# One table of tokens by expert split into two, the first block's rows turned later, and the probabilities stored as 18 rows

## The chip, the core and the metric

The kernel runs on one core of one Trainium2 chip. A core has TensorE (PE, matmuls and transposes), VectorE (DVE), ScalarE (ACT), GpSimd (POOL) and SyncE (SP), which here only issues DMAs and loads registers. Each takes its own instructions strictly in the order in which the program hands them out and waits on the others by semaphores. The metric is the device time of one execution in microseconds.

## The reference

Three stages follow one another: attention with pooled queries, a mixing layer with a gate, and a routed layer in which each token goes to one of eight experts.

```python
def _moe2_ref(x, w_gate, w_local, w1, w2):        # x: (4, 576, 512)
    logits = np.einsum('bsd,de->bse', x, w_gate)
    local_gate = 1.0 / (1.0 + np.exp(-np.einsum('bsd,de->bse', x, w_local).squeeze(-1)))
    for b in range(B):
        prev_e = -1
        for s in range(S):
            fresh_e = int(np.argmax(logits[b, s]))
            if s == 0 or local_gate[b, s] < 0.5:
                e = fresh_e
            else:
                e = prev_e if prev_e >= 0 else fresh_e
            prev_e = e
            p = ...                               # softmax of logits[b, s]
            h = np.maximum(x[b, s] @ w1[e], 0.0)
            out[b, s] = p[e] * (h @ w2[e])
```

Before it, `_attn_ref` averages pairs of queries and computes softmax(q k / 8) v, and `_moe_ref` mixes each token with the one before it, computes relu(xk w_k) squared times w_v, and multiplies by sigmoid(xr w_r). There are 2304 tokens of 512 numbers.

## The kernel before

The attention comes first and is not touched but for its constants. The 2304 tokens of the mixing layer are worked in 9 pairs `u` of tiles of 128 tokens. From u = 2 to u = 7 a loop does one round each: `hidden(u+1, 0..1)`, `gate(u, 0)`, `route2(u-1)`, the mixing of pair u+2, `value(u, 0)`, `product(u, 0)`, `route3(u-1)`, `logits(u, 0)`, `gate(u, 1)`, `route4(u-1)`, `value(u, 1)`, `product(u, 1)`, `logits(u, 1)`, `hidden(u+1, 2..3)`, `route1(u)`. The pair u = 8 is written out behind the loop.

Routing: `logits` are nine multiply-and-add passes on DVE (line 783). `route1` (DVE) takes the largest logit and makes `kg` (line 822), the gate and candidate of each token; `route2` turns `kg` into a row on PE (line 832), ACT copies it to `krow` (line 836), and a scan on DVE gives the expert of every token as `erow` (line 838). `route3` spreads it on PE (line 849) and DVE makes the one-hot `oh` (line 850). `route4` counts with matmuls of `oh` (lines 857 to 861), DVE adds up the slots to `base` (lines 863 to 869), and POOL writes the token numbers `tid` of the two tiles into the DRAM table `tbl` by two indirect DMAs (line 871). The table has a list of 2816 places for each expert; places not written hold 2304, an index that means "no token". A hidden group's squares go from ACT (lines 745 to 747) to POOL, which makes the low half (line 748); the low half of the mixed tokens is POOL's as well (line 568).

The routed layer goes in blocks of up to 512 tokens of one expert. `early()` takes the expert with the most tokens of the first 14 tiles as block 0, before the routing is complete. For a block, `load_ids` (line 1015, SP) loads 512 token numbers from the table, `gather_x` (lines 1027, 1029, POOL) fetches these tokens' rows by indirect DMA, two tiles of 128 at a time, `transpose_x` turns them on PE (line 1054) with copies by ACT and DVE (lines 1057, 1058), `load_w` and `split_w` load 8 pieces of weights and split them into a high and a low half (lines 988, 994; 1010, 1011), and `up`/`down` multiply (lines 1068, 1085). `gather_p` (line 1037, POOL) fetches the tokens' probabilities from the DRAM tensor `pd`, which `probabilities()` writes: 18 numbers on each of 128 partitions, as single numbers (line 1217). `finish` (lines 1093, 1094) scales and stores.

SP's DMAs run on a set of eight completion counters, used in turn; an issue can thus wait for the DMA eight issues before it. Ahead of block 1 SP loads the registers of all later blocks, 28 register loads between the store of the probabilities and the next weights.

## Time and profile before

| | |
|---|---|
| three runs | 1199.29, 1200.1 (median), 1203.38 us |
| profiled execution | 1199.74 us, its span 1198.0 us |
| PE busy | 1080.2 us (90% of the span) |
| DVE, ACT, POOL busy | 828.2, 718.6, 575.3 us |
| mean granted TensorE clock, whole span | 0.972 of full speed |
| the same from 830 to 870 us, 870 to 910, 910 to 950 | 0.85, 0.90, 0.91 |
| the same from 950 to 1070 us | 1.00 |

The views in order of time give the start and length of merged instructions, and in square brackets how long the engine sat idle before the first of them and what ended that. The view of waits adds the same idle times up by the pair of instructions. Idle time of an engine costs only where PE, the busiest one, or the end of the program waits for it in turn.

### The profile page before, as it was taken

The numbers are of one execution on the slowest core, as the hardware profiler recorded it, in microseconds if no ns is written. First come the engines' busy times: TensorE is split into PE (matmuls) and PEld (weight loads), VectorE is DVE, ScalarE is ACT, GpSimd is POOL, SyncE is SP. The second block draws the span as 40 slices with busy tenths as digits, with TensorE's granted clock in tenths as the row PEclk, the third lists the DMA queues.
The fourth block names the chain that finished last, engine by engine and source line by source line (L and its number), as shares of the span: only waits on it lengthen the run. The fifth ranks groups of instructions, "written<-read, shape, count | busy, mean of one in ns | idle before, by whom it ended". The sixth has DMA issues, their size and how long they took to land. (4 is left out here: it accounts for less than half of the span.)

```text
span 1198.0 us, 18084 instructions
## 1 busy us (share of the span) xinstructions
PE 1080.2 (90%) x6073; PEld 910.6 (76%) x6073; DVE 828.2 (69%) x1255; ACT 718.6 (60%) x1006; POOL 575.3 (48%) x392
## 2 busy tenths in 40 slices
PE   7899999999999999978999989897987999998875
PEld 6677777777777777767887878776776888876764
DVE  6888888888888888889955665685353544446544
ACT  5787777777777777767775444341333535446543
POOL 2556666666666666468734333342213514144233
PEclk9999999999999999998999999998897999999988
DMA  9166666656566564515520322203646756556765
GB/s 198 32 132 148 138 142 141 140 130 131 131 149 141 137 138 100 157 45 172 182 98 10 36 31 32 36 18 89 117 81 153 253 178 202 176 179 213 251 205 176
DMA packets 147348, 156.31 MB, mean 130 GB/s; under 512 B 62993, under 2 KB 115857, under 8 KB 146324
## 3 DMA queue, kind: packets, MB, share of 16 engines
q1 hardware_dynamic: 140836, 141.51, 47.4%
q0 software_dynamic: 6384, 13.15, 3.7%
q8 instruction: 73, 1.20, 0.5%
q14 instruction: 55, 0.45, 0.1%
HBM read 107.30 MB, written 15.58 MB: 103 GB/s over the span
## 5 line engine op out<-in xcount | busy, mean ns | idle before, releaser
L403 PE MATMUL pvt<-sr,V 128*128 128x288 f32 x1152 | 328.5, 409 | 31.4 <-ACT xc L416 14.7
L403 PEld LDWEIGHTS pvt<-sr,V 128*128 128x128 f32 x1152 | 202.1, 190 | 71.2 <-POOL sr L389 17.9
L345 PE MATMUL pt<-kw 128*128 128x288 f32 x1152 | 247.3, 337 | 5.5 <-DVE Mt L357 4.1
L389 POOL TENSOR_TENSOR sr<-sr,Mb 128x576 f32<-128x576 f32 x96 | 142.5, 1487 | 195.3 <-ACT Mb L380 159.5
L357 DVE TENSOR_TENSOR Mt<-Mt,pt 128x576 f32<-128x576 f32 x224 | 168.1, 750 | 76.2 <-ACT sr L349 74.3
L349 ACT ACTIVATE sr<-pt 128x576 f32<-128x576 f32 x288 | 181.5, 646 | 54.6 <-PE pt L345 52.4
L345 PEld LDWEIGHTS pt<-kw 128*128 128x128 f32 x1152 | 177.6, 189 | 34.8 <-DVE Mt L357 10.4
L396 ACT ACTIVATE sr<-sr 128x1728 f32<-128x1728 f32 x96 | 157.9, 1644 | 52.0 <-DVE sr L390 46.4
L390 DVE TENSOR_TENSOR sr<-sr,Mb 128x1152 f32<-128x1152 f32 x96 | 160.9, 1676 | 2.8 <-ACT Mb L380 2.8
L727 PE MATMUL ph<-a,wk 128*128 128x256 f32 x864 | 108.4, 286 | 0.9 <-ACT kr L745 0.4
L727 PEld LDWEIGHTS ph<-a,wk 128*128 128x128 f32 x864 | 106.5, 193 | 2.6 <-ACT kr L745 1.0
L767 PE MATMUL py<-kw,sq 128*128 128x512 f32 x312 | 84.3, 423 | 0.0
L1068 PE MATMUL ph<-a,wk 128*128 128x256 f32 x576 | 73.4, 288 | 6.3 <-PEq L1415 5.8
L1085 PE MATMUL py<-kw,sq 128*128 128x512 f32 x324 | 78.3, 398 | 0.0
L1068 PEld LDWEIGHTS ph<-a,wk 128*128 128x128 f32 x576 | 71.3, 195 | 8.8 <-issue 7.7
L871 POOL DMA_INDIRECT tbl<-tid,si x18 | 18.4, 1021 | 122.9 <-DMA tbl<-tid,si 67.2
L745 ACT ACTIVATE kr<-ph 128x512 f32<-128x512 f32 x36 | 21.3, 592 | 92.4 <-PE ph L727 57.2
L446 POOL TENSOR_TENSOR xo<-xc,t 64x576 f32<-64x576 f32 x32 | 73.1, 2283 | 1.2
L783 DVE CUSTOM_DVE_ANT_0 a<-r,wg 128x512 f32<-128x512 f32 x96 | 71.4, 744 | 3.1
L767 PEld LDWEIGHTS py<-kw,sq 128*128 128x128 f32 x312 | 62.1, 203 | 15.0 <-issue 0.2
L1085 PEld LDWEIGHTS py<-kw,sq 128*128 128x128 f32 x324 | 60.8, 189 | 14.5
L1037 POOL DMA_INDIRECT pg<-pd,ids x44 | 44.4, 1009 | 37.4 <-DMA pg<-pd,ids 15.7
(250 smaller groups left out, 1756.7 us busy)
## 6 DMA issues: line engine op xcount, KB each, us to landing
wraw<-in_moe_w_dram SPq DMA_DIRECT2D x101, 512.0 KB
kw<-Hk SPq DMA_DIRECT2D x224, 72.0 KB
ql<-in_q_dram SPq DMA_DIRECT2D x16, 576.0 KB
kl<-in_k_dram SPq DMA_DIRECT2D x64, 144.0 KB
V<-in_v_dram SPq DMA_DIRECT2D x128, 72.0 KB
kw<-Hq SPq DMA_DIRECT2D x112, 72.0 KB
kw<-kw SPq DMA_DIRECT2D x14, 576.0 KB
xTd<-xo SPq DMA_DIRECT2D x16, 288.0 KB
```

The costliest lines, as they stand in the source:

```text
L345: nc.tensor.matmul(pt[:, i, :HT], lhsT=lhs, rhs=qh[:, hl, hd, i, :], start=(hl == 0), stop=(hl == 1))
L349: nc.scalar.activation(out=Sg[h, kt], in_=ptt[h, kt][:, :, :HT], func=AF.Copy)
L357: nc.vector.tensor_tensor(out=Mt[h], in0=a, in1=pt[:, :, :HT], op=ALU.max)
L389: nc.gpsimd.tensor_tensor(out=s[:, 0], in0=s[:, 0], in1=Mb[h], op=ALU.subtract)
L390: nc.vector.tensor_tensor(out=s[:, 1:3], in0=s[:, 1:3], in1=Mb[h].unsqueeze(1).to_broadcast([P, 2, T]), op=ALU.subtract)
L396: nc.scalar.activation(out=s, in_=s, func=AF.Exp, scale=scale)
L403: nc.tensor.matmul(pvt[h][:, i, :HT], lhsT=V[(h // 2) % 2][:, kt, c : c + P], rhs=Sg[h, kt][:, i], start=(kt == 0), stop=(kt == KT - 1),)
L446: nc.gpsimd.tensor_tensor(out=xo[p].rearrange("p (i t c) -> p i c t", i=2, c=9)[a], in0=y[a], in1=t2[a], op=ALU.mult)
L727: nc.tensor.matmul(pt[:, i], lhsT=wk[:, wl, g, c, P * i : P * i + P], rhs=a[:, xl, c], start=(n == 0), stop=(n == 11))
L767: nc.tensor.matmul(p_v, lhsT=SQ[u, f // 2][:, xl, f % 2, s], rhs=wv[:, wl, f], start=(f == 0 and n == 0), stop=(f == 7 and n == 2),)
L1068: nc.tensor.matmul(pt[:, i], lhsT=w[:, wl, g, c, P * i : P * i + P], rhs=x[:, xl, c], start=(n == 0), stop=(n == 11))
L1085: nc.tensor.matmul(py[i], lhsT=hs[:, xl, f, P * i : P * i + P], rhs=w[:, wl, 2 * g + f], start=(g == 0 and n == 0), stop=(g == 3 and n == 5),)
```

## The change

There are two DRAM tables, `tbl[0]` for the even tiles of a pair and `tbl[1]` for the odd ones. Table 0 is filled with 2304, table 1 with 0, and the token numbers of odd tiles are stored less 2304, so the sum of the two tables is the list of before. `load_ids` loads both lists, the second into one of two new tiles `idb`, and POOL adds them in front of a block's first gather. The turning of block 0's first rows and the gather of its other rows move from in front of `route2` of pair 7 to behind `product(8, 0)`. The probabilities are turned on PE into 18 rows of 128 numbers, copied by DVE and stored as rows; this store is issued behind the last products of block 0's first half instead of ahead of POOL's gathers.

```diff
     xTd = dram.tile([DM, NTOK], F32, name="xTd")
     x2d = dram.tile([NTOK + 1, DM], F32, name="x2d")
     pd = dram.tile([NTOK + 1, 1], F32, name="pd")
-    tbl = dram.tile([E * NTS, 1], I32, name="tbl")
+    tbl = [dram.tile([E * NTS, 1], I32, name=f"tbl{i}") for i in range(2)]
 
     ctx.enter_context(tc.manual_schedule())
 
...
     nks = cp.tile([1, 8], I32, name="nks")
     wgt = cp.tile([P, 4, E + 1], F32, name="wgt")
     ids = [cp.tile([P, 4], I32, name=f"ids{i}") for i in range(4)]
+    idb = [cp.tile([P, 4], I32, name=f"idb{i}") for i in range(2)]
     pgs = [cp.tile([P, 4], F32, name=f"pg{i}") for i in range(2)]
 
     io = dict(allow_small_or_imprecise_dtypes=True)
...
         nc.gpsimd.iota(im8, pattern=[[1, E]], base=-E, channel_multiplier=0, **io)
         nc.gpsimd.iota(base, pattern=[[NTS, E]], base=0, channel_multiplier=0, **io)
         nc.gpsimd.iota(base0, pattern=[[NTS, E]], base=0, channel_multiplier=0, **io)
-        nc.gpsimd.iota(tid, pattern=[[P, NT]], base=0, channel_multiplier=1)
+        nc.gpsimd.iota(
+            tid.rearrange("p (u i) -> p u i", i=2), pattern=[[2 * P, NU], [P - NTOK, 2]], base=0, channel_multiplier=1
+        )
         nc.gpsimd.iota(k128, pattern=[[-P, 4 * NK]], base=0, channel_multiplier=0, **io)
         nc.gpsimd.iota(i4, pattern=[[1, 4]], base=1, channel_multiplier=0, **io)
         nc.gpsimd.iota(cc, pattern=[[1, NC]], base=0, channel_multiplier=0, **io)
...
         nc.vector.tensor_scalar(out=om, in0=mus, scalar1=-1.0, scalar2=1.0, op0=ALU.mult, op1=ALU.add)
         pad = tp.tile([P, E * NTS // P], I32, name="pad")
         nc.gpsimd.memset(pad, NTOK)
-        nc.sync.dma_start(tbl.rearrange("(p f) o -> p (f o)", p=P), pad)
+        nc.sync.dma_start(tbl[0].rearrange("(p f) o -> p (f o)", p=P), pad)
+        pad0 = tp.tile([P, E * NTS // P], I32, name="pad0")
+        nc.gpsimd.memset(pad0, 0)
+        nc.sync.dma_start(tbl[1].rearrange("(p f) o -> p (f o)", p=P), pad0)
         z = tp.tile([1, DM], F32, name="z")
         nc.gpsimd.memset(z, 0.0)
         nc.sync.dma_start(x2d[NTOK : NTOK + 1, :], z)
...
         nc.vector.tensor_tensor(out=base, in0=base, in1=p3[:, 2], op=ALU.add)
         for i in range(2):
             nc.gpsimd.indirect_dma_start(
-                out=tbl, out_offset=bass.IndirectOffsetOnAxis(ap=si[:, i : i + 1], axis=0),
+                out=tbl[i], out_offset=bass.IndirectOffsetOnAxis(ap=si[:, i : i + 1], axis=0),
                 in_=tid[:, 2 * u + i : 2 * u + i + 1], in_offset=None,
             )
 
...
 
     def load_ids(j):
         if j <= JX:
-            nc.sync.dma_start(
-                ids[j % 4], tbl[bass.ds(regs[j][1], 512), :].rearrange("(i p) o -> p (i o)", p=P),
-                allow_slow_non_contiguous=True,
-            )
+            for t, to in zip(tbl, (ids[j % 4], idb[j % 2])):
+                nc.sync.dma_start(
+                    to, t[bass.ds(regs[j][1], 512), :].rearrange("(i p) o -> p (i o)", p=P),
+                    allow_slow_non_contiguous=True,
+                )
 
 
     def gather_x(j, t):
         if j > JX:
             return
+        if t == 0:
+            nc.gpsimd.tensor_tensor(out=ids[j % 4], in0=ids[j % 4], in1=idb[j % 2], op=ALU.add)
         for i in range(2):
             ix = bass.IndirectOffsetOnAxis(ap=ids[j % 4][:, t + i : t + i + 1], axis=0)
             if j:
...
         pe = rp.tile([P, NT], F32, name="pe")
         nc.vector.tensor_reduce(out=pe, in_=ls, axis=AX.X, op=ALU.add)
         nc.vector.tensor_tensor(out=pe, in0=pe, in1=sm, op=ALU.mult)
-        nc.sync.dma_start(
-            pd[0:NTOK].rearrange("(t p) o -> p (t o)", p=P), pe, allow_slow_non_contiguous=True
-        )
+        return pe, ls
+
+
+    def store_p(pe, ls):
+        nc.tensor.transpose(p23[0:NT, 0:P], pe, ident)
+        row = ls.rearrange("p t e -> p (t e)")[0:NT, 0:P]
+        nc.vector.tensor_copy(row, p23[0:NT, 0:P])
+        nc.sync.dma_start(pd[0:NTOK].rearrange("(t p) o -> t (p o)", p=P), row)
 
 
     def first_block():
...
 
     u = NU - 1
     gate(u, 0, py[0])
-    transpose_x(0)
-    gather_x(0, 2)
     route2(u - 1)
     split_w(0)
     load_w(3)
...
     route3(u - 1)
     value(u, 0, py[1], range(4, 8))
     product(u, 0, py[1])
+    transpose_x(0)
+    gather_x(0, 2)
     split_w(1)
     load_w(4)
     gate(u, 1, py[0])
...
         load_w(s)
     load_ids(1)
     load_ids(2)
-    probabilities()
+    pe, ls = probabilities()
     gather_x(1, 0)
+    down(0, 2)
+    down(0, 3)
+    store_p(pe, ls)
     gather_p(0, 0)
     gather_p(0, 2)
-    down(0, 2)
-    down(0, 3)
     n0 = nc.values_load(lst0[:, 2:3], min_val=0, max_val=512)
     nk = [nc.values_load(nks[:, i : i + 1], min_val=0, max_val=JX) if i != 4 else None for i in range(8)]
     for j in range(3, JX + 1):
```

The places where the order moves, before and then after the change. POOL, from the fill of the first block's rows to the scatter of pair 7 (`tbl` is the table, `ids` and `idb` the lists, `xg` the gathered rows, `sq` squares), before:

```order
L1264 MEMSET xg_4333 128x1024
L871 DMA tbl<-tid,si 22528x1 x2
L1029 DMA xg_4333<-x2d,ids_97 128x512 x2
L748 TENSOR_TENSOR sq_4894<-kr_4889,sq_4894 128x512
L748 TENSOR_TENSOR sq_4895<-kr_4890,sq_4895 128x512
L1029 DMA xg_4333<-x2d,ids_97 128x512 x2
L871 DMA tbl<-tid,si 22528x1 x2
```

The same stretch of POOL after the change:

```order
L1278 MEMSET xg_4339 128x1024
L877 DMA tbl_60<-tid,si 22528x1
L877 DMA tbl_61<-tid,si 22528x1
L1032 TENSOR_TENSOR ids_98<-ids_98,idb_102 128x4
L1038 DMA xg_4339<-x2d,ids_98 128x512 x2
L754 TENSOR_TENSOR sq_4900<-kr_4895,sq_4900 128x512
L754 TENSOR_TENSOR sq_4901<-kr_4896,sq_4901 128x512
L1038 DMA xg_4339<-x2d,ids_98 128x512 x2
L877 DMA tbl_60<-tid,si 22528x1
L877 DMA tbl_61<-tid,si 22528x1
```

The two scatters have two targets now, and the add of the lists is new; the rest keeps its order.

PE, from the first gate of pair 8 to its second (`py` of line 758 is the gate, of line 767 the value products), before:

```order
L758 MATMUL py_4751<-wr,a_4899 128x512 x12
L1054 MATMUL ptx_4884<-ident,xg_4333 128x128 x4
L1054 MATMUL ptx_4885<-ident,xg_4333 128x128 x4
L832 LDWEIGHTS kg
...
L767 MATMUL py_4752<-kw,sq_4887 128x512 x6
L767 MATMUL py_4752<-kw,sq_4888 128x512 x6
...
L767 MATMUL py_4752<-kw,sq_4894 128x512 x6
L767 MATMUL py_4752<-kw,sq_4895 128x512 x6
L758 MATMUL py_4751<-wr,a_4899 128x512 x12
```

The same stretch of PE after the change (line 764 is the gate, 773 the value products, 1063 the transposes):

```order
L764 MATMUL py_4757<-wr,a_4905 128x512 x12
L838 LDWEIGHTS kg
...
L773 MATMUL py_4758<-kw,sq_4893 128x512 x6
L773 MATMUL py_4758<-kw,sq_4894 128x512 x6
...
L773 MATMUL py_4758<-kw,sq_4900 128x512 x6
L773 MATMUL py_4758<-kw,sq_4901 128x512 x6
L1063 MATMUL ptx_4890<-ident,xg_4339 128x128 x4
L1063 MATMUL ptx_4891<-ident,xg_4339 128x128 x4
L764 MATMUL py_4757<-wr,a_4905 128x512 x12
```

The eight transposes moved behind the routing of pair 7 and 24 value matmuls.

SP, from the last weight piece ahead of the lists to the register loads (`wraw` is a weight piece, `pd` the probabilities), before:

```order
L994 DMA wraw_4332<-in_moe_w_dram 128x2x512
L1015 REGISTER_ALU
L1015 DMA ids_98<-tbl 128x4x1
L1015 REGISTER_ALU
L1015 DMA ids_99<-tbl 128x4x1
L1217 DMA pd<-pe 128x18x1
L1355 TENSOR_LOAD lst_93
```

The same stretch of SP after the change:

```order
L1000 DMA wraw_4338<-in_moe_w_dram 128x2x512
L1022 REGISTER_ALU
L1022 DMA ids_99<-tbl_60 128x4x1
L1022 REGISTER_ALU
L1022 DMA idb_103<-tbl_61 128x4x1
L1022 REGISTER_ALU
L1022 DMA ids_100<-tbl_60 128x4x1
L1022 REGISTER_ALU
L1022 DMA idb_102<-tbl_61 128x4x1
L1233 DMA pd<-ls 18x128
L1370 TENSOR_LOAD lst_94
```

Two list loads became four, and the store writes 18 rows of 128 numbers.

## Rows read from the trace of the kernel before

**Rows 1.** which waits held PE from 620 to 960 us: total, times, longest

```profile
PE ptx L1054 <- DMA xg<-x2d,ids: 12.3, 4, 7.0
PE p L857 <- DVE oh L850: 7.8, 4, 3.9
```

**Rows 2.** the same view from 960 us to the end, its longest row

```profile
PE ph L1120 <- issue: 7.3, 2, 6.6
```

**Rows 3.** PE in order of time: start, length, operation, idle before it

```profile
671.08 2.93 PE L758 MATMUL py<-wr,a 128*128 128x512 f32 x12
```

**Rows 4.** the same view further on, two gates and a wait

```profile
700.81 2.93 PE L758 MATMUL py<-wr,a 128*128 128x512 f32 x12
...
717.76 0.17 PE L857 MATMUL p<-oh,trib 128*128 128x8 bf16 x1 [3.85 <-DVE oh L850]
```

**Rows 5.** PE again, the gate that opens the last round

```profile
800.25 2.93 PE L758 MATMUL py<-wr,a 128*128 128x512 f32 x12
```

**Rows 6.** POOL in order of time, a second scatter

```profile
700.34 0.96 POOL L871 DMA_INDIRECT tbl<-tid,si  x1 [6.72 <-DMA tbl<-tid,si]
```

**Rows 7.** ACT in order of time, the square behind it

```profile
705.02 0.60 ACT L745 ACTIVATE kr<-ph 128x512 f32<-128x512 f32 x1 [7.78 <-POOL kw L748]
```

**Rows 8.** DVE in order of time, one logit beside POOL's work

```profile
797.64 5.53 DVE L783 CUSTOM_DVE_ANT_0 a<-r,wloc 128x512 f32<-128x512 f32 x1
```

**Rows 9.** POOL in that stretch, first and last of three

```profile
797.73 2.41 POOL L568 TENSOR_TENSOR a<-m,a 128x1024 fp32r<-128x1024 f32 x1
...
801.33 1.29 POOL L748 TENSOR_TENSOR sq<-kr,sq 128x512 fp32r<-128x512 f32 x1
```

**Rows 10.** page, costliest groups: logits, busy time and mean ns of one

```profile
L783 DVE CUSTOM_DVE_ANT_0 a<-r,wg 128x512 f32<-128x512 f32 x96 | 71.4, 744 | 3.1
```

**Rows 11.** PE after that stretch

```profile
805.09 0.47 PE L832 MATMUL p<-identb,kg 128*1 128x128 bf16 x4 [1.90 <-DVE kg L822]
...
807.54 2.79 PE L767 MATMUL py<-kw,sq 128*128 128x512 f32 x6
```

**Rows 12.** PE at the first block's transposes

```profile
837.23 0.45 PE L1054 MATMUL ptx<-ident,xg 128*128 128x128 f32 x1 [7.00 <-DMA xg<-x2d,ids]
...
840.14 4.89 PE L767 MATMUL py<-kw,sq 128*128 128x512 f32 x12
...
845.10 3.07 PE L767 MATMUL py<-kw,sq 128*128 128x512 f32 x12
```

**Rows 13.** POOL before them: the second scatter and the gather

```profile
819.50 1.38 POOL L871 DMA_INDIRECT tbl<-tid,si  x1 [6.24 <-DMA tbl<-tid,si]
829.49 1.03 POOL L1029 DMA_INDIRECT xg<-x2d,ids  x1 [8.61 <-issue]
```

**Rows 14.** SP's DMA issues there

```profile
825.19 0.41 SPq L1015 DMA_DIRECT2D ids<-tbl  x1
```

**Rows 15.** PE around the second block's transposes

```profile
888.00 5.91 PE L1068 MATMUL p<-a,wk 128*128 128x256 f32 x48
899.44 8.73 PE L1068 MATMUL p<-a,wk 128*128 128x256 f32 x48 [5.53 <-DVE kw L1075]
912.87 0.45 PE L1054 MATMUL ptx<-ident,xg 128*128 128x128 f32 x1 [4.70 <-DMA xg<-x2d,ids]
...
915.53 2.93 PE L1085 MATMUL py<-kw 128*128 128x512 f32 x6
```

**Rows 16.** ACT in that stretch

```profile
896.47 1.06 ACT L1010 ACTIVATE w1b<-wraw 128x1024 fp32r<-128x1024 f32 x1 [4.12 <-DMA wraw<-in_moe_w_dram]
```

**Rows 17.** DVE, the last operation of the probabilities

```profile
885.79 0.18 DVE L1216 TENSOR_TENSOR pe<-pe,sm 128x18 f32<-128x18 f32 x1
```

**Rows 18.** SP's issues: probabilities, then the next weights

```profile
897.25 0.50 SPq L1217 DMA_DIRECT2D pd<-pe  x1
915.50 4.76 SPq L994 DMA_DIRECT2D wraw<-in_moe_w_dram  x3
```

**Rows 19.** POOL, the second block's gather

```profile
901.72 0.98 POOL L1027 DMA_INDIRECT xg<-x2d,ids  x1 [14.24 <-DMA ids<-tbl]
```

## The prediction

> **What bounds the kernel now.** I read the page's shares first: TensorE (PE) is the busiest engine, so a gain has to be PE idle time or slow PE time. Then the view of PE's waits by stretch. From 620 to 960 us PE waits for data: 12.3 us for gathered rows before transposes, 7.8 us for the one-hot rows of the routing (oh) [rows 1]. From 960 us to the end its longest wait is on instruction issue, not on data [rows 2]. So what PE gains before 960 us should reach the end of the span one for one.
>
> Then the views in order of time. The loop over pairs of token tiles goes in rounds; I take the gate matmuls that open each as marks. One round lasted from 671.08 to 700.81 us, 29.7 us with almost no idle time [rows 3, 4]; I call this the clean round. From 671.08 to 800.25 us are four rounds [rows 3, 5]: 129.2 us, 32.3 each, so 2.6 us are lost per round. The reader is to follow the loss of one round backwards: PE waits 3.85 us for oh [rows 4]; the second scatter into the table sat 6.72 us on POOL until the first had landed [rows 6]; POOL's halves of the squares stand behind it in order, and ACT's next activation waited 7.78 us for such a one to free its buffer [rows 7]; the routing row and the mixing stand behind that on ACT, and oh behind the mixing on DVE.
>
> **The change part by part.** *A. Two tables.* The second scatter goes to another table, so it waits no more. POOL's low half of the mix and its squares then run some 7 us earlier. What is late next? They now fall beside DVE's logits. The trace has one such case: a logit that takes 0.74 us on average lasted 5.53 us while POOL did three operations from 797.73 to 802.62 us [rows 8 to 10], and PE then waited 1.90 us for the gate row kg; the next six matmuls took 2.79 us [rows 11] where half of twelve undisturbed ones is 1.5 us [rows 12], so that stop cost 3.2 us in all. DVE stood still as long as POOL worked.
>
> The Trainium skill says this as a rule (SBUF — State Buffer, section "Who interferes with whom"): a DVE instruction with two SBUF inputs contends with a GpSimd instruction that reads SBUF, and one of them blocks whole. This case's logit of 5.53 us agrees. The rule speaks against this edit, since it makes each earlier POOL operation a stop of the logits; what that comes to at worst is the second and third rival below.
>
> How late is kg? From the end of a round's last value matmul PE has four groups of 24 hidden matmuls (two take 5.91 us [rows 15]) and a gate of 2.93 us [rows 3] before it wants kg: 14.7 us. DVE has in that time a product, nine logits of 0.74 us and seven small reductions, some 8.5 us undisturbed. POOL has one operation of 2.41 us and three or four of 1.29 us [rows 9]: 6.3 to 7.6 us. If each stops DVE, kg comes after 14.8 to 16.1 us, 0.1 to 1.4 us late; the only row of such a stop says 1.90 us. I take 1.3 us, between them, and no slow matmuls behind it. So a round gains 2.6 - 1.3 = 1.3 us, and over the six rounds (u = 2 to 7) 7.5 us. Bounds: 6 x 2.6 = 15.5 us if nothing is late, and 6 x (2.6 - 3.2) = -4 us at the price of that row.
>
> *B. The first block's transposes move behind the last pair's first product.* PE waited 7.00 us in front of them, and the twelve matmuls behind took 4.89 us where the next twelve took 3.07 us [rows 12]: 7.0 + 1.8 = 8.8 us. The rows must then be there when PE comes: routing and 24 value matmuls behind the gate, about 6.5 us later than now, at 836.7 us on the old clock. They landed at 837.23 us, but the second scatter (819.50 us, after 6.24 us of waiting [rows 13]) now goes out beside the first; the list is loaded at 825.19 us now [rows 14] and can be some 5 us earlier, less 0.4 us for the second list's load. The add of the two lists stands on POOL before the gather: at most a 128x512 operation, 1.29 us [rows 9], at least nothing; 0.4 us, since it has 4 elements per row. So the rows land near 833 us and PE waits for nothing. Queued behind that add and two gathers on POOL (1.03 us [rows 13] each) stand two squares; they now fall on the last logits' reductions and can make kg up to 2.6 us late, or not at all: I charge 1.3. B is worth 7.5 us; bounds 4.9 (2.6 us late and slow matmuls as in rows 11) and 8.8.
>
> *C. The second block's list, and the probabilities.* PE waited 5.53 us at 899.44 us, because ACT's split of a weight piece waited for its landing until 896.47 us and stands before the block's activations [rows 15, 16]. That stays: nothing in the change moves it. Then PE waited 4.70 us for the gathered rows, and six matmuls behind took 2.93 us [rows 15], 1.4 us too long. This goes: the gather ran at 901.72 us after 14.24 us for its list [rows 19], which waited for the last scatter; the second scatter there goes 8 us earlier too. I charge 1 us because the two lists, now loaded twice, fetch their single numbers among the weight pieces that ACT waits for. C = 4.7 + 1.4 - 1 = 5 us; bounds 6 and 0 (the weight pieces late by as much).
>
> The probabilities are ready at 885.97 us [rows 17] and PE ends its products before 888.00 us [rows 15], so one more transpose (the 128x128 ones there take 0.45 us [rows 15] at the most) waits for nothing. SP's store waits for DMA slots: with the added loads it comes behind the same weight landing, 896.47 us, so it is issued about where it was, 897.25 us [rows 18]. SP's register loads behind it, and the weights at 915.50 us [rows 18], therefore move only with the shift of A and B. These weights are wanted behind a whole block's products and the next block's first matmuls, some 18 us after 915.5 us; 5 us of this can be spent.
>
> Nothing I charge for the rest: one more fill and store at the start (an issue of 0.50 us like [rows 18] on SP while PE works from loaded tiles), and per block an added load on SP and an add on POOL, both ahead of a gather for a later block. If that cover is gone, each block pays 0.4 + 0.4 us, 12 blocks 10 us.
>
> Sum: 7.5 + 7.5 + 5 = 20 us. The profiled execution took 1199.74 us (span 1198.0), so 1179.7 us; the median before, 1200.1 us, is 0.4 us higher. I say **1180 us**.
>
> **The rivals.**
> 1. *POOL's work finds gaps.* The operations in SBUF do not stop DVE often, because ACT hands over the squares between logits. For it: in the clean round PE stood still for almost nothing. Against: the 5.53 us. All upper bounds: 15.5 + 8.8 + 6 = 30 us, 1169 us.
> 2. *The stop costs what it cost once.* Each round loses 1.90 us and the slow matmuls behind: A = -4, B = 4.9, C = 5: 6 us, 1194 us. For it: the one row; against: there POOL's three operations came in one piece at the end of the logits.
> 3. *Slower: DVE and POOL in series.* If all of POOL's work in a round (four squares of 1.29, two of 2.41 us: 10 us) stops DVE's chain from kg to kg (two sets of logits 13.3 us, mixing, scan, products and small steps some 9.5 us), a round lasts 32.8 us, and with slow matmuls behind each wait (1.3 to 1.8 us) over 34. Against the 32.3 us of now A is then -11 to -14 us; B loses its transposes' gain to the same late kg (0), and C keeps little. It decides from 34 us a round: 1199.7 + 12 - 5 = 1207 us. Against it: half of POOL's work falls where DVE waits anyway.
> 4. *The two tables do not run side by side*, or C is lost to the weight pieces: then B or A with B alone, 12 to 15 us, 1186 us.
>
> **How the numbers follow.** About 0.3%, 3.6 us, is what can be told from no change. Chances: forecast (1174 to 1187 us) 0.52, rival 1 0.17, rival 2 0.16, rival 3 0.04, rival 4 0.11. Faster: 0.52 + 0.17 + 0.11 and most of rival 2, 0.92; same 0.04; slower 0.04. The range for 8 in 10 reaches from rival 1 to near rival 2: 1168 to 1192 us; the forecast's own is 1174 to 1187.
>
> **What would show it.** A: no wait of a scatter for a scatter on POOL; PE's waits for oh gone from the rounds, waits for kg of 0 to 2 us in their place, rounds of about 31 us between gates. B: the transposes after the product with under 0.5 us of waiting; the gate to second gate stretch shorter by 7 us or more. C: no wait for gathered rows at the second block, the wait of 5 us before it still there. It is wrong if rounds are not shorter than 32 us, if PE waits for rows in the new place, or if the stretch from 960 us on gives time back.

## The result, and the profile after

The changed kernel takes 1171.82 us (median of 4 runs, 1169.44 to 1174.48) against 1199.69 us (4 runs, 1199.13 to 1203.38) for the kernel before on the same chip: ratio 0.9762, 95% interval 0.9731 to 0.9793, a gain of 28 us where 20 were forecast. Measured once more, beside other runs of the kernel before (last section of the experiments), the ratio is 0.9817, a gain of 22 us, so the size of the gain is known only to some 6 us. The first time lies under the forecast's own range (1174 to 1187 us) and inside the wide one (1168 to 1192 us). The profiled execution took 1174.48 us, the longest of the four; its span is 1172.3 us against 1198.0 us: 25.7 us less. All lengths below come from these two spans, in which the same instructions are used as marks.

The first view is PE's waits from 620 to 960 us of the changed kernel (what waited, for what, us in all, times, longest); it answers to [rows 1].

```profile
PE p L838 <- DVE kg L828: 7.3, 4, 2.2
PE p L1138 <- ACT kr L1133: 3.6, 1, 3.6
PE ptx L1063 <- DMA xg<-x2d,ids: 2.1, 2, 1.1
```

The waits for oh are gone and those for rows (xg) fell from 12.3 to 2.1 us. Waits for kg remain, and there is a new one on ACT's kr.

PE in order of time shows where. First the rounds: the gates that open rounds u = 2, 3, 4 and 7, and the two waits for kg.

```profile
637.88 2.92 PE L764 MATMUL py<-wr,a 128*128 128x512 f32 x12
...
667.35 2.92 PE L764 MATMUL py<-wr,a 128*128 128x512 f32 x12
671.80 0.47 PE L838 MATMUL p<-identb,kg 128*1 128x128 bf16 x4 [1.52 <-DVE kg L828]
...
698.28 2.92 PE L764 MATMUL py<-wr,a 128*128 128x512 f32 x12
...
732.16 0.47 PE L838 MATMUL p<-identb,kg 128*1 128x128 bf16 x4 [1.54 <-DVE kg L828]
...
787.95 2.92 PE L764 MATMUL py<-wr,a 128*128 128x512 f32 x12
```

The rounds now alternate, 29.5 and 30.9 us, where they lasted 32.3 us on average [rows 3 to 5]; kg is late in every other one only. On POOL the second scatter of a round goes out 1.3 us behind the first and waits for no landing, where it had waited 6.72 us [rows 6]:

```profile
717.86 0.99 POOL L877 DMA_INDIRECT tbl<-tid,si  x1 [8.47 <-DVE base L875]
719.16 1.38 POOL L877 DMA_INDIRECT tbl<-tid,si  x1 [0.30 <-issue]
```

Then the first block's transposes, in their new place, and the gate behind them (to [rows 12]):

```profile
816.46 0.47 PE L838 MATMUL p<-identb,kg 128*1 128x128 bf16 x4 [2.01 <-DVE kg L828]
816.86 4.61 PE L773 MATMUL py<-kw,sq 128*128 128x512 f32 x12
...
824.45 1.03 PE L1063 MATMUL ptx<-ident,xg 128*128 128x128 f32 x8
825.24 3.00 PE L764 MATMUL py<-wr,a 128*128 128x512 f32 x12
```

The transposes wait for nothing, but the 7.00 us wait has a small heir in front of it: 2.01 us for kg, with twelve products of 4.61 us behind. "Slow" products or matmuls are, here and below, the same instructions at a lower granted clock: these twelve ran at 0.62 of full speed, and the next twelve, at 1.00, took 3.08 us.

Then the second block (to [rows 15]):

```profile
866.68 6.00 PE L1077 MATMUL p<-a,wk 128*128 128x256 f32 x48 [1.37 <-issue]
873.02 6.01 PE L1077 MATMUL p<-a,wk 128*128 128x256 f32 x48 [0.34 <-DVE kw L1084]
880.08 0.30 PE L1063 MATMUL ptx<-ident,xg 128*128 128x128 f32 x1 [1.04 <-DMA xg<-x2d,ids]
881.47 1.41 PE L1063 MATMUL ptx<-ident,xg 128*128 128x128 f32 x7 [1.09 <-DMA xg<-x2d,ids]
882.53 2.90 PE L1094 MATMUL py<-kw 128*128 128x512 f32 x6
...
904.44 1.14 PE L1138 MATMUL p<-ident,kr 128*128 128x128 f32 x8 [3.61 <-ACT kr L1133]
```

The 5.53 us wait is 0.34 us and the second 48 products take 6.01 us instead of 8.73 (granted clock 1.00 and 0.64); the wait for rows is 2.1 us instead of 4.70. The last row is where some of it is given back. The marks give the account of the 25.7 us:

| stretch of PE | before | after | difference |
|---|---|---|---|
| start to gate of round u = 2 | 637.13 | 637.88 | +0.75 |
| rounds u = 2 to 7 (to the gate of pair 8) | 190.16 | 173.65 | -16.5 |
| pair 8, first gate to second gate | 20.71 | 13.71 | -7.0 |
| second gate to the second block's first products | 40.00 | 41.44 | +1.4 |
| from there to its first down product behind the transposes | 27.53 | 15.85 | -11.7 |
| from there to the next block's first up products | 27.45 | 32.36 | +4.9 |
| the rest | 255.0 | 257.4 | +2.4 |

The ends of the first rows before are these two gates:

```profile
637.13 2.93 PE L758 MATMUL py<-wr,a 128*128 128x512 f32 x12
...
827.29 2.93 PE L758 MATMUL py<-wr,a 128*128 128x512 f32 x12
```

### The profile page after: what moved, and what is told of

Read it like the earlier page. It is cut to its first block, busy times and chain, and to the rows that moved or that the text cites. A ratio compares the mean times of both kernels' runs of the same rounds, so it can differ in the third digit from the quotient of the medians.

```text
span 1172.3 us, 18157 instructions
## 1 busy us (share of the span) xinstructions
PE 1075.8 (92%) x6074; PEld 908.0 (77%) x6074; DVE 847.6 (72%) x1256; ACT 720.0 (61%) x1006; POOL 583.6 (50%) x406
## 5 line engine op out<-in xcount | busy, mean ns | idle before, releaser
L395 POOL TENSOR_TENSOR sr<-sr,Mb 128x576 f32<-128x576 f32 x96 | 142.5, 1487 | 195.9 <-ACT Mb L386 170.3
L789 DVE CUSTOM_DVE_ANT_0 a<-r,wg 128x512 f32<-128x512 f32 x96 | 93.7, 976 | 3.1
L773 PE MATMUL py<-kw,sq 128*128 128x512 f32 x312 | 79.5, 405 | 0.0
L1094 PE MATMUL py<-kw,sq 128*128 128x512 f32 x324 | 77.9, 397 | 0.0
L1094 PEld LDWEIGHTS py<-kw,sq 128*128 128x128 f32 x324 | 60.6, 188 | 14.3
L773 PEld LDWEIGHTS py<-kw,sq 128*128 128x128 f32 x312 | 58.7, 192 | 13.9
L574 POOL TENSOR_TENSOR a<-m,a 128x1024 fp32r<-128x1024 f32 x18 | 44.1, 2450 | 42.1 <-ACT a L573 37.2
L1046 POOL DMA_INDIRECT pg<-pd,ids x44 | 44.7, 1016 | 29.6 <-DMA pg<-pd,ids 16.5
```

The source lines that it names most:

```text
L395: nc.gpsimd.tensor_tensor(out=s[:, 0], in0=s[:, 0], in1=Mb[h], op=ALU.subtract)
L773: nc.tensor.matmul(p_v, lhsT=SQ[u, f // 2][:, xl, f % 2, s], rhs=wv[:, wl, f], start=(f == 0 and n == 0), stop=(f == 7 and n == 2),)
L789: nc.vector.tensor_tensor_reduce(out=a32, in0=x2, in1=wg[:, e] if e < E else wloc, scale=1.0, scalar=0.0, op0=ALU.mult, op1=ALU.add, accum ...
L1094: nc.tensor.matmul(py[i], lhsT=hs[:, xl, f, P * i : P * i + P], rhs=w[:, wl, 2 * g + f], start=(g == 0 and n == 0), stop=(g == 3 and n == 5),)
```

## The experiments

The kernels went to the chip in three groups, each beside runs of the kernel before there (medians 1195.1, 1196.8 and 1197.9 us): the first four, the next four, and the last three of the sections below. I compare ratios to these: the times in the expectations were reckoned from some 1200 us, 2 to 5 us above these medians. The changed kernel's own two ratios, 0.9762 and 0.9817, lie 6 us apart, so a smaller difference between kernels of different groups is read from the traces alone. In the traces I compare three stretches of PE: **rounds** (gate of u = 2 to gate of pair 8), **pair 8** (its first gate to its second), and **block stretch** (second block's first up products to the transposes `p<-ident,xg` two blocks on). Single executions of kernels with one table differ in the rounds, 185.6 to 190.2 us, with the same code there; the seven profiles of kernels with two tables and the same order of work there lie between 173.6 and 174.0 us.

| kernel | ratio to before | rounds | pair 8 | block stretch |
|---|---|---|---|---|
| before | 1 | 190.2 | 20.7 | 69.3 |
| changed | 0.9762 (0.9731 to 0.9793) | 173.7 | 13.7 | 62.6 |
| tables alone | 0.9814 (0.9766 to 0.9862) | 173.7 | 14.7 | 65.3 |
| move alone | 0.9935 (0.9907 to 0.9963) | 187.8 | 11.4 | 69.4 |
| row store alone | 0.9963 (0.9935 to 0.9991) | 188.4 | 20.6 | 64.4 |
| tables and move | 0.9814 (0.9778 to 0.985) | 173.7 | 12.1 | 66.5 |
| changed, registers late | 0.9746 (0.9729 to 0.9764) | 173.7 | 13.7 | 59.7 |
| before, registers late | 1.0013 (0.9991 to 1.0034) | 185.6 | 20.7 | 70.5 |
| changed, mix first | 0.9815 (0.9788 to 0.9841) | 173.1 | 12.2 | 63.6 |
| changed, last pair in one table | 0.98 (0.9776 to 0.9824) | 173.7 | 12.2 | 67.7 |
| three edits | 0.9708 (0.968 to 0.9736) | 173.7 | 10.8 | 56.8 |
| three edits, and in the rounds | 0.9717 (0.9692 to 0.9743) | 175.2 | 10.8 | 55.8 |
| changed, run again | 0.9817 (0.9792 to 0.9843) | 174.0 | 13.6 | 63.2 |

### The tables alone

```diff
-    tbl = dram.tile([E * NTS, 1], I32, name="tbl")
+    tbl = [dram.tile([E * NTS, 1], I32, name=f"tbl{i}") for i in range(2)]
...
-                out=tbl, out_offset=bass.IndirectOffsetOnAxis(ap=si[:, i : i + 1], axis=0),
+                out=tbl[i], out_offset=bass.IndirectOffsetOnAxis(ap=si[:, i : i + 1], axis=0),
```

with the second list's load and the add; transposes and store as before.

> The kernel before with the two tables alone (second table, list sums on GpSimd); transposes and the store of the probabilities as before. Theory (from the two traces): the tables carry A, -16.5 us, and most of the second block's gain, because the scatter that used to be in flight beside the weight pieces lands before they are issued: PE's wait of 5.53 us in the second block falls under 1 us. The list of the first block also lands some 6 us earlier, so PE's wait for gathered rows in the old place falls from 7.0 to 1 to 3 us. Sum -16.5 - 5 - 11.7 + 4.9 given back = some -26 to -28 us: 1172 to 1176 us. Rival 1 (the row store frees the weight landing, not the tables): the wait of 5.53 us stays, 1178 to 1182 us. Rival 2 (my forecast's sizes): A -7.5, C -5, 1182 to 1188 us.

Measured: 1174.4 us, by the ratio 22 us less than before, where 26 to 28 were expected. PE at the transposes in the old place and in the second block:

```profile
818.62 0.98 PE L1063 MATMUL ptx<-ident,xg 128*128 128x128 f32 x7 [2.88 <-DMA xg<-x2d,ids]
...
874.26 6.01 PE L1077 MATMUL p<-a,wk 128*128 128x256 f32 x48 [0.95 <-DVE kw L1084]
888.76 0.45 PE L1063 MATMUL ptx<-ident,xg 128*128 128x128 f32 x1 [8.48 <-DMA xg<-x2d,ids]
```

The theory holds for the rounds, the first block (2.88 us) and the 5.53 us wait (0.95). The rows of the second block it did not foresee: PE waits 8.48 us for them, not less but more than before. POOL's view says what was under way then:

```profile
877.42 0.99 POOL L1036 DMA_INDIRECT xg<-x2d,ids  x1 [0.63 <-POOL ids L1032]
...
887.21 0.94 POOL L1046 DMA_INDIRECT pg<-pd,ids  x1 [7.54 <-DMA pd<-pe]
```

The store of 2304 single numbers, issued at 873.94 us, landed at about 887.2 us, 13.3 us later, and the gather of 877.42 us was there for PE only at 888.76 us, 11.3 us after its issue.

### The move alone

```diff
     gate(u, 0, py[0])
-    transpose_x(0)
-    gather_x(0, 2)
     route2(u - 1)
...
     product(u, 0, py[1])
+    transpose_x(0)
+    gather_x(0, 2)
```

> The kernel before with only the transposes and the second gather of block 0 moved behind the last pair's first product. Theory: the step stands alone, its rows land at some 837 us and PE comes at about that time, so PE's 7.0 us wait and the slow matmuls behind it go and under 1.5 us of waiting is left: -6 to -8 us, 1192 to 1194 us. Rival (the move needs the earlier list, so it is worth something only together with the tables): rows still late in the new place, PE waits 3 us or more there, under -4 us, 1196 us or more.

Measured: 1186.62 us against 1195.13 us, 7.8 us by the ratio. The move does not need the tables. Pair 8 is 11.4 us between its gates, and the transposes wait for nothing:

```profile
834.29 1.36 PE L1054 MATMUL ptx<-ident,xg 128*128 128x128 f32 x8
835.40 2.98 PE L758 MATMUL py<-wr,a 128*128 128x512 f32 x12
```

Beside the tables it is worth less, since the tables alone had brought the rows sooner, and kg is late there by 2.0 us: 14.7 us fell to 13.6 or 13.7 us in three kernels (changed, the same run again, registers late) and to 12.1 or 12.2 us in three others with the same code in pair 8 (tables and move, mix first, last pair in one table). What parts them is the granted clock behind the wait for kg: the twelve products there took 4.4 to 4.6 us in the first three (0.62 in the changed kernel) and 3.1 us in the others (1.00).

### The row store alone

```diff
-        nc.sync.dma_start(
-            pd[0:NTOK].rearrange("(t p) o -> p (t o)", p=P), pe, allow_slow_non_contiguous=True
-        )
+        nc.tensor.transpose(p23[0:NT, 0:P], pe, ident)
+        row = ls.rearrange("p t e -> p (t e)")[0:NT, 0:P]
+        nc.vector.tensor_copy(row, p23[0:NT, 0:P])
+        nc.sync.dma_start(pd[0:NTOK].rearrange("(t p) o -> t (p o)", p=P), row)
```

and the gathers of probabilities behind the last products.

> The kernel before with only the probabilities stored as 18 rows behind the first half's last products. Theory: the weight piece of 896.47 us landed before the old store of 2304 single numbers was even issued, so the store cannot have delayed it and the 5.53 us wait stays (over 4 us); the new transpose costs PE an issue stop of some 1.4 us, the gathers of probabilities come later but still before they are wanted: 0 to +2 us, 1199.5 to 1202 us. Rival (the single numbers of the store are what held the transfers up): PE's wait of 5.53 us falls under 2 us, -4 us or more, 1196 us or less.

Measured: 1191.32 us against 1195.13 us, by the ratio 4.4 us less (interval 1 to 8 us). That is the rival's time, but neither side had the reason. The middle wait is 3.39 us, less than the theory's 4 and more than the rival's 2, and what went is a wait that neither named. (The profiled execution took 1199.25 us, one of the longest of the twelve: it shows where PE waits, not the gain of the median.)

```profile
897.12 8.71 PE L1068 MATMUL p<-a,wk 128*128 128x256 f32 x48 [3.39 <-DVE kw L1075]
905.67 0.60 PE L1054 MATMUL ptx<-ident,xg 128*128 128x128 f32 x4
907.24 0.66 PE L1054 MATMUL ptx<-ident,xg 128*128 128x128 f32 x4 [0.98 <-DVE sq L1075]
```

The 4.70 us for gathered rows are gone. So the store of single numbers, not the second scatter, is what the rows of the second block had waited for.

### The changed kernel without the row store

The edit is the reverse of the last one, made to the changed kernel.

> The changed kernel with the probabilities stored as before (2304 single numbers, ahead of GpSimd's gathers of probabilities). Theory: the row store costs PE an issue stop of 1.4 us and brings nothing, so this kernel takes 1169 to 1172 us, the same as or up to 2 us under the changed one, and PE's second-block wait stays under 1 us. Rival (the row store is what cleared the second block): the wait of 5 us comes back, 1175 to 1180 us.

Measured: 1173.13 us, ratio 0.9814, which the two measurements of the changed kernel (0.9762 and 0.9817) do not tell apart from it. So the time decides nothing. By the trace neither side was right: the wait of 5 us did not come back (1.34 us), and the row store does bring something.

```profile
870.35 6.02 PE L1077 MATMUL p<-a,wk 128*128 128x256 f32 x48 [1.34 <-DVE kw L1084]
884.61 0.45 PE L1063 MATMUL ptx<-ident,xg 128*128 128x128 f32 x1 [8.24 <-DMA xg<-x2d,ids]
```

PE waits 8.24 us for rows here and 2.1 us in the changed kernel. But the next weights go out 18.4 and 18.5 us behind the store of the probabilities (888.41 and 891.21 us): whoever is early at the rows waits for weights afterwards. The issue stop of 1.4 us ahead of the second block comes with the row store in all profiles that have it, and in none without. In sum the block stretch is 3.3 to 4.0 us shorter with the row store (62.6 and 63.2 us against 66.5), and the stop in front of it takes 1.4 us back.

### Registers loaded late, in the changed kernel and in the one before

```diff
-    for j in range(3, JX + 1):
-        block_regs(j, lst[:, 0, j - 1 : j], lst[:, 1, j - 1 : j])
...
     def block(j):
+        if j + 2 <= JX:
+            block_regs(j + 2, lst[:, 0, j + 1 : j + 2], lst[:, 1, j + 1 : j + 2])
         load_ids(j + 2)
```

> The changed kernel with the register loads for blocks 3 and later taken out of the row of 28 that SP does ahead of the next weights; each block loads the registers of the block after next as its first step. Theory: what the changed kernel gives back behind the second block (+4.9 us, PE's wait of 3.61 us and slow matmuls) comes from those weights, issued at 891.21 us, 18.5 us behind the store of the probabilities; with 20 of 28 loads gone they go out some 13 us earlier, ACT's wait of 9.42 us and PE's 3.61 us go, -4 to -6 us: ratio to before 0.971 to 0.973, some 1166 us. Rival (the weights wait for a free buffer or a DMA slot, not for the loads): they are issued within 3 us of where they were, no change (1171 to 1173 us).

> The kernel before with the same edit to the register loads alone. Theory: there PE came to the second block's down products 20 us after the weights' issue would allow, because it waited 4.70 us for gathered rows first, so the loads were hidden and the edit brings 0 to -1.5 us: 1198.5 to 1200 us. Rival (the register loads cost in any case): -4 us or more, 1196 us or less.

Measured: 1167.09 us (ratio 0.9746, where 0.971 to 0.973 was expected) and 1198.17 us (1.0013). SP's issues, in the changed kernel, and with late registers:

```profile
863.31 2.22 SPq L994 DMA_DIRECT2D wraw<-in_moe_w_dram  x4
...
872.70 1.12 SPq L1233 DMA_DIRECT2D pd<-ls  x1
891.21 2.21 SPq L1000 DMA_DIRECT2D wraw<-in_moe_w_dram  x3
```

```profile
872.19 0.93 SPq L1233 DMA_DIRECT2D pd<-ls  x1
878.31 11.34 SPq L1000 DMA_DIRECT2D wraw<-in_moe_w_dram  x3
```

The weights go out 6.1 us behind the store and not 18.5, and the wait on kr is gone: the theory. The gain shows in the block stretch, 59.7 us against 62.6 and 63.2; the ratio is not clear of the changed kernel's first one (0.9762). PE's rows pay part of it, since the weights now run into the gathers:

```profile
882.42 1.75 PE L1063 MATMUL ptx<-ident,xg 128*128 128x128 f32 x7 [2.56 <-DMA xg<-x2d,ids]
```

In the kernel before the edit brings nothing, and the same effect is plain: PE's wait for these rows rose from 4.70 to 9.39 us, with the weights issued at 895.71 us and the gather at 896.54 us.

```profile
909.69 2.30 PE L1054 MATMUL ptx<-ident,xg 128*128 128x128 f32 x8 [9.39 <-DMA xg<-x2d,ids]
```

### GpSimd's second low half ahead of the scatters

```diff
-        if u + 2 < NU:
-            route4(u - 1)
         if u + 2 < NU:
             mix_split(u + 2, 1)
+        if u + 2 < NU:
+            route4(u - 1)
```

> The changed kernel with GpSimd's second low half of the mix issued ahead of the two scatters instead of behind them, so it runs some 8 to 11 us earlier in a round, beside the first set of logits and not the second. Theory (a GpSimd operation stops the logits it runs beside, wherever that is, and DVE's whole chain from kg to kg is the bound): a logit of 2 to 3 us appears in the first set, the 3 to 4.3 us logit of the second set becomes short, rounds stay at 29.5 to 30.5 us: within 3 us of the changed kernel, 1169 to 1174 us. Rival (only stops behind the last product cost): PE's wait for kg of 1.5 us in every other round goes, -3 to -5 us, 1167 to 1169 us.

Measured: 1174.03 us, no gain. First the changed kernel, DVE's longest logit of a round and what POOL did then:

```profile
720.49 4.30 DVE L789 CUSTOM_DVE_ANT_0 a<-r,wg 128x512 f32<-128x512 f32 x1
```

```profile
720.57 2.41 POOL L574 TENSOR_TENSOR a<-m,a 128x1024 fp32r<-128x1024 f32 x1
722.93 3.01 POOL L754 TENSOR_TENSOR sq<-kr,sq 128x512 fp32r<-128x512 f32 x2
```

Then the same two engines in the experiment:

```profile
712.28 2.77 DVE L789 CUSTOM_DVE_ANT_0 a<-r,wg 128x512 f32<-128x512 f32 x1
```

```profile
711.80 2.70 POOL L574 TENSOR_TENSOR a<-m,a 128x1024 fp32r<-128x1024 f32 x1 [2.64 <-ACT a L573]
```

The stop follows the operation into the first set of logits, and the rounds last what they lasted (173.1 us): the theory. The kg waits are 1.24 us, where the rival wanted them gone.

### The last pair's scatters in one table

```diff
-                out=tbl[i], out_offset=bass.IndirectOffsetOnAxis(ap=si[:, i : i + 1], axis=0),
+                out=tbl[i if u < NU - 1 else 0], out_offset=bass.IndirectOffsetOnAxis(ap=si[:, i : i + 1], axis=0),
```

with the last tile's token numbers stored without the shift.

> The changed kernel with both scatters of the last pair alone sent to the first table, so that the second waits for the first again and is in flight beside the second block's weight pieces. Theory (that scatter is what made the first weight pieces late): the second piece lands some 10 us behind the issue of the weights and not 7, PE's wait in the middle of the second block's up products rises from 0.34 us to 3 to 6 us, and the gathered rows come later too: +4 to +9 us over the changed kernel, 1176 to 1181 us. Rival (the pieces came late for another reason): that wait stays under 1.5 us, the pieces land 5 and 7 us behind their issue, and only the gathered rows are later by the scatter's landing.

Measured: 1174.15 us, ratio 0.98. POOL's second scatter, ACT's first weight piece and PE's wait:

```profile
859.16 0.97 POOL L878 DMA_INDIRECT tbl<-tid,si  x1 [6.85 <-DMA tbl<-tid,si]
```

```profile
868.55 1.06 ACT L1017 ACTIVATE w1b<-wraw 128x1024 fp32r<-128x1024 f32 x1 [10.05 <-DMA wraw<-in_moe_w_dram]
870.02 1.06 ACT L1017 ACTIVATE w1b<-wraw 128x1024 fp32r<-128x1024 f32 x1 [0.42 <-DMA wraw<-in_moe_w_dram]
```

```profile
872.99 7.50 PE L1078 MATMUL p<-a,wk 128*128 128x256 f32 x48 [3.18 <-DVE kw L1085]
```

The wait is back, 3.18 us with slow products behind it. The weights went out at 860.42 us; ACT took the second piece 9.6 us later. That interval is 9.0 to 10.1 us in the five kernels in which a scatter goes out within 1.5 us of the weights (before, move alone, row store alone, before with late registers, this one), and 5.3 to 6.7 us in the eight in which both scatters went out some 8 us before the weights. So what is beside the weights decides, which is the theory. The time shows less: it is under the expected 1176 to 1181 us, and by the ratios +4.5 us over the first measurement of the changed kernel and -2 us over the second (+4 to +9 us were expected). The block stretch is 67.7 us against 62.6 and 63.2; the wait for rows, expected to grow, did not.

### A faster version: three edits, and a fourth

The edits to the changed kernel: registers of blocks 6 and later late; the transpose of the probabilities between the last products; six value products of pair 8 ahead of its routing row. The fourth puts six value products ahead in the rounds as well.

```diff
-    for j in range(3, JX + 1):
+    for j in range(3, 6):
         block_regs(j, lst[:, 0, j - 1 : j], lst[:, 1, j - 1 : j])
...
     def block(j):
+        if 6 <= j + 2 <= JX:
+            block_regs(j + 2, lst[:, 0, j + 1 : j + 2], lst[:, 1, j + 1 : j + 2])
...
     gate(u, 0, py[0])
+    value(u, 0, py[1], range(2))
     route2(u - 1)
     split_w(0)
     load_w(3)
-    value(u, 0, py[1], range(4))
+    value(u, 0, py[1], range(2, 4))
...
-    down(0, 3)
+    down(0, 3, (0,))
     store_p(pe, ls)
+    down(0, 3, (1,))
```

and for the fourth, in the loop:

```diff
         gate(u, 0, py[0])
+        if u + 2 < NU:
+            value(u, 0, py[1], range(2))
         route2(u - 1)
...
-            value(u, 0, py[1])
+            value(u, 0, py[1], range(2, 8))
```

> The changed kernel with three edits meant to beat it: the registers of blocks 6 and later loaded late (14 of the 28 loads moved, not 20, so that the next weights go out near 882 us, behind the landing of the second block's gathered rows); the transpose of the probabilities between the two halves of the last products; and PE's first six value products of pair 8 put ahead of its routing row, where PE waited 2.01 us for kg and the next twelve products took 4.61 us. Theory: the gathers' wait of 2.56 us that the kernel with 20 loads moved has falls to about 1 us, the issue stop of 1.37 us goes, and 2 to 3.5 us come from the routing row: 1161 to 1165 us, 5 to 10 us under the changed kernel. Rival (what PE saves there it waits for in the second block, whose weights hang on DVE's and SP's chain, not on PE): no better than the kernel with 20 loads moved, 1166 to 1169 us.

> The kernel with the three edits, and in the rounds too PE does six value products ahead of the routing row. Theory (DVE's chain, longer by GpSimd's stops, is the bound over two rounds, so PE's wait of 1.5 us in every other round only shows it): rounds stay at 30.0 us on average, the time is within 2 us of the kernel with the three edits. Rival (PE's order is the bound, and the wait is lost time): the waits for kg go, rounds fall to 29.3 to 29.5 us, -3 to -5 us.

> The changed kernel as it is, beside these two on the same chip, so that they can be compared with it: ratio to before 0.974 to 0.979, second-block weights issued 18.5 us behind the store of the probabilities.

Measured on one chip: 1162.21 us with three edits, 1163.49 us with four, 1175.27 us for the changed kernel; the intervals of the first and the last do not touch. The three edits bring 13 us by these medians, where 5 to 10 were expected, and 8 us by the profiled spans. PE with three edits:

```profile
816.71 0.47 PE L838 MATMUL p<-identb,kg 128*1 128x128 bf16 x4 [0.63 <-DVE kg L828]
...
864.26 11.77 PE L1077 MATMUL p<-a,wk 128*128 128x256 f32 x96 [1.42 <-issue]
876.62 0.30 PE L1063 MATMUL ptx<-ident,xg 128*128 128x128 f32 x1 [0.58 <-DMA xg<-x2d,ids]
878.39 0.98 PE L1063 MATMUL ptx<-ident,xg 128*128 128x128 f32 x7 [1.47 <-issue]
```

Against the changed kernel run again, pair 8 is 2.9 us shorter and the block stretch 6.4 us: the theory for the routing row and the weights, which go out at 882.90 us. Of the 2.9 us some 1.3 are the granted clock: behind kg that kernel's twelve products took 4.40 us, at 0.66. The wait for rows is 0.58 us, with 1.47 us of idle time put down to issue behind it. The transpose's edit failed: the issue stop is still 1.42 us with six products behind the transpose, and the trace does not name what ends it; that stays open.

With the fourth edit the rounds are no shorter, as the theory has it. PE's wait for kg only became one for oh:

```profile
650.76 0.17 PE L863 MATMUL p<-oh,trib 128*128 128x8 bf16 x1 [1.30 <-DVE oh L856]
...
672.54 0.47 PE L838 MATMUL p<-identb,kg 128*1 128x128 bf16 x4 [0.15 <-DVE kg L828]
```

The changed kernel run again gave 0.9817, just above the range that I had set for it, and its weights went out 21.7 us behind the store where 18.5 were expected.

## Why the prediction was right, and where it was not

In the profiles 25.7 us came: 16.5 from A, 7.0 from B and 5.4 from C, less 0.8 at the start and 2.4 in the rest. A was forecast 9 us too small, B nearly right by two misses that offset each other, and C right by luck.

**A, two tables: right in kind, 9 us too small in size.** The mechanism was as told: no scatter waits for a scatter, DVE's logits are stopped by POOL, kg is late. The logits show the stop over the whole kernel (groups of the profile's page: busy time, mean ns of one):

```profile
L789 DVE CUSTOM_DVE_ANT_0 a<-r,wg 128x512 f32<-128x512 f32 x96 | 93.7, 976 | 3.1
```

71.4 us at 744 ns before [rows 10], 93.7 us at 976 ns now. Two terms were mis-sized. "2.6 us are lost per round" was a mean over the four rounds in the middle; the first round lasted 33.95 us and the last lost some 3.5 us. Without any loss the six would last 170.3 us (five of 29.35 us and the last of 23.6), so 19.8 us were there to win and not 15.5. And "I take 1.3 us [...] over the six rounds" charged 7.8 us for kg (six times 1.3; the 7.5 us left over in the sum should be 7.8 too), where it is 1.5 us in two of the six, with the next products at full speed (3.3 us with what stands behind): DVE's chain takes about 30 us (two rounds now last 60.4 us) and PE's 29.3, so the delay adds up over two rounds before PE feels it. 19.8 - 3.3 = 16.5 us. This profile of the kernel before has the longest rounds of four with the same loop (185.6 to 190.2 us); against the shortest, A is 12 us, still more than forecast. The upper bound of 15.5 us was no bound, because its rounds were picked. That kg's wait only shows DVE's chain is what the fourth edit and the mix-first kernel showed. The price of 3.2 us for the one stop of the kernel before was too small as well: between the two rows of [rows 11] stand six more products that took 1.99 us instead of 1.5, so it was 3.7 us.

**B, the move: 7.0 us against 7.5.** The step charged 1.3 us for kg and expected no wait for rows. Rows were there; kg cost 2.01 us and 1.5 us of slow products, more than charged, within the bound of 2.6 us and slow products. The slow products came in some kernels only, as told above. Against that stands a term that the step left out: the eight transposes behind the old wait were slow too, 2.4 us from the first to the matmuls behind them, and take 0.8 us now (1.1 with the move alone). So alone the move makes the stretch 9.3 us shorter, above my bound of 8.8.

**C: 5 us forecast; 11.7 us came and 4.9 and 1.4 went, 5.4 us in all, and the reasons were wrong.** That the sum comes out near 5 us is luck. Of its own two terms, 4.7 us of waiting and 1.4 us of slow matmuls, 2.9 us came (both waits for rows together, 5.05 us before, are 2.13) and nothing (the six products still take 2.90 us); most of the 11.7 us is the wait that was to stay and the slow products behind it. Three sentences failed.
- "That stays: nothing in the change moves it", of the 5.53 us wait. The tables moved it: the second scatter was in flight when the weights were issued, 886.50 and 886.35 us in the kernel before. The tables alone take the wait to 0.95 us, and one table for the last pair alone brings 3.18 us back.
- "This goes: the gather ran at 901.72 us after 14.24 us for its list", of the rows. The list did come sooner: with the tables alone the gather goes out 10.0 us behind the block's first products, 13.7 us before. But PE, rid of the 5.53 us wait, comes 7.3 us sooner too, and the wait grows. What was late and stayed late is the gather itself. The row of PE in [rows 15] and the gather in [rows 19] are 11.2 us apart, and the first block's gather took 7.7 us [rows 12, 13]; that difference could be read beforehand. The store of single numbers [rows 18] was beside it. With tables and that store the wait is 8.24 to 8.48 us; with the row store alone it is gone. The Trainium skill (DMA: Bandwidth & Descriptors, sections "Rules for kernel authors" and "Issuing engines are not separate DMA queues") says that a transfer whose last dimension isn't contiguous becomes one descriptor per number and that transfers from all issuing engines interleave on the same 16 DMA engines. The traces agree: from 865 to 915 us they count 5979 and 6007 packets under 512 bytes in the two kernels with tables and that store, 3731 in the changed kernel (2304 numbers less 18 rows are 2286); and the store took 13.3 us and the gather beside it 11.3 us, where the gather takes 4.0 us in the changed kernel.
- "5 us of this can be spent", of the weights behind SP's register loads. They could not: ACT waited 9.42 us and PE 3.61 us for them. Loading registers late took that wait away in the changed kernel and did nothing in the kernel before.

```profile
896.59 1.06 ACT L1016 ACTIVATE w2b<-wraw 128x1024 fp32r<-128x1024 f32 x1 [9.42 <-DMA wraw<-in_moe_w_dram]
```

The row store's own price, 1.4 us of issue stop, was put at nothing. The rest of the span, +2.4 us, I put down to no edit: from the transposes `p<-ident,xg` to the end it is 240.7 us before, 243.1 after, and 240.2 in the changed kernel run again; over all profiles it lies between 238.1 and 245.4 us. In the changed kernel two groups of 24 matmuls there (its line 1129) are 1.9 and 0.9 us longer than before, at a granted clock of 0.64 and 0.67 against 1.00 and 0.77.

**The signs.** Those of A and B came as told: rounds under 31 us, kg late by 0 to 2 us, the pair 7.0 us shorter, transposes that wait for nothing. Those of C did not: a wait for rows of 2.1 us is left, and the wait of 5 us before it is gone. Of the three signs of being wrong one came, and weakly: time was given back, 4.9 us of it ahead of 960 us of the old clock, by the weights, and 2.4 us behind, within what the profiles differ by.

**The rivals.** The first (1169 us) had the sum nearly, but not its reason: POOL's work did not find gaps. The second and third fell with the rounds: a stop in the logits delays DVE, but not PE by as much. The fourth's first half is answered by the tables alone, where the scatters go out 1.3 us apart; its second half came in part, since 4.9 of C's 11.7 us went to the weights of the block behind.

## What to carry to other kernels

A transfer's length from issue to landing is to be compared with others of its kind in the same trace; where it is long, look at what else was in flight, above all transfers of single numbers. A bound for what can be won in a loop is taken over all its rounds, not over the ones in the middle. When a stretch becomes faster, ask what stands in program order on each issuing queue between here and the next thing wanted: here it was a row of register loads that had cost nothing before.

## What the hardware showed that I had not expected

- 2304 numbers stored singly took 13.3 us to land (tables alone), and made a gather beside them take 11.3 us; as 18 rows beside the same work the gather took 4.0 us.
- One indirect scatter of 128 single numbers beside weight loads of 512 KB cost the second weight piece some 3 to 4 us (9.0 to 10.1 us from issue to use, against 5.3 to 6.7).
- The stops between DVE and POOL go both ways. In the changed kernel a POOL square that falls beside logits is longer too:

```profile
755.24 1.76 POOL L754 TENSOR_TENSOR sq<-kr,sq 128x512 fp32r<-128x512 f32 x1 [1.41 <-ACT kr L753]
```

where a square took 1.29 us before [rows 9]. DVE's logit that had begun at 755.15 us, ahead of the square, lasted its usual 0.69 us; the one behind it, begun at 755.88 us, took 1.66 us.
